# One product with ones per chunk, and output projections in fp16 parts, in a layer kernel on one core

## The chip, the cores and the metric

The kernel runs on one core of a Trainium2 chip. The core has TensorE (PE, matrix products; its weight loads are listed apart as PEld), VectorE (DVE), ScalarE (ACT), GpSimd (POOL) and the queues of SyncE (SP), from which most transfers are issued. The metric is the device time of one execution in microseconds. All times below are microseconds unless marked otherwise.

## What is computed

Two branches share one normalised input and are added to it (S = 2048 tokens, width D = 512):

```
xn = layernorm(x)
q = (xn @ wq) in 32 heads of 16;  k = xn @ wk;  v = xn @ wv      # one k and v for all heads
A  = concat_heads(softmax(q k^T / 4) v) @ wo                      # the output projection
s1, s2 = scores of xn against two sets of 64 keys, 32 heads       # product keys
top 2 of each, top 2 of the 4 sums, softmax g, expert index e
B  = sum over heads and 2 experts of g * gelu(xn . u[e]) * v[e]   # 4096 experts
out = x + A + B
```

For each token, branch B chooses 64 experts. Its choice must be the reference's, so the score products are exact to about fp32.

## The kernel before

**Split products.** A value that must stay near fp32 is scaled by a power of two and written as an fp16 high part plus an fp16 low part. ACT writes the high part (a copy with a scale), and DVE writes the low part (`scalar_tensor_tensor`: value times scale minus high part). One product of 128 x 128 x 512 is then three fp16 products into the same PSUM tile, the pairs (high, high), (high, low), (low, high) of `TERMS`. The queries, keys, scores and dense experts are done so. The power of two comes from `factors` (three integer operations on DVE) on a sum of squares. That sum is made with a product with a matrix of ones, which adds over the 128 partitions.

**The score weights.** The weights of the expert scores come in 8 chunks (`wp_make`), each of 4 parts. `wp_square` puts the squares of part n into one column of `squares` (128 x 4). `wp_factors` (L620 to L628) then adds the four columns with four fp32 products with ones, each with one moving column, into one PSUM column `pn`. ACT scales that by `K2`, and `factors` makes the chunk's scale. This happens 8 times, at 36 to 304 us.

**Attention.** Four query blocks of 512 tokens, in the order QB = (0, 1, 3, 2), times 8 groups of 4 heads, make 32 units. A unit runs over the 2048 keys in 16 pieces. For each piece PE makes scores (`sc`, L451), ACT their exponentials (`pt`, L458), and PE the product with the values and a column of ones (`pv`, L468, fp32). One step `d` of the main loop does two pieces; there are 256 steps, and `i` = 2d counts pieces. Two units are a pair `pp` (0 to 15). `unit_tail` copies the sums out, transfers place the rows in `ot` and the divisors in DRAM, `pair_load`, `pair_invert` and `pair_spread` invert and spread the divisors as `rs`, and `pair_tail` (L514 to L518), at remainder 12 of the next pair, multiplies `ot` by `rs` on DVE (L517). The product `on` has 128 rows of the attention output, fp32, transposed. Four pairs make one query block.

**Output projection.** `load_wo` fetches the weights `wo` (two tiles of 512 KB, fp32) once per query block. `block_out` (L562 to L576) multiplies 128 tokens: four fp32 products with `on` as weights and `wo` moving (L568), then DVE adds the PSUM tile to the token tile's total (L572). Twelve such blocks serve the first three query blocks of the order. The fourth is done at the end by `last_out_a` and `last_out_b`.

**Experts.** For half of the tokens, rows of u and v are gathered by index (POOL, L1194). For each row DVE makes a product with the token (L1206) and adds the weighted v row (L1241). For the other half (two groups of 512 tokens) the gates are spread into dense matrices by one-hot products (L988 to L1035), and all 4096 experts are run as dense products (`pact` L930, `pout` L1072).

**The order of the work.** It is written out in the program: the loop issues every engine's instructions step by step, and each engine runs its own in that order. In a step come the first two score products and exponentials, `pv`, then `mid()`, the other two scores, perhaps one `block_out`, and `fill()`. In `mid()`, functions put on `ON_ACT` in the step before or at the start of the step run on ACT, and functions put on `BEHIND` run on DVE among the sums of gathered rows. `store(...)` puts a transfer off to the start of the next step, on SP's queue. `fill()` runs the generator of the score and dense work (`score_thread`), which states a charge for each piece of work (`UNIT` = 0.235 per fp16 product, 3.6 per block). The generator is run until its charges reach an aim that rises evenly over the 256 steps to `FILL`. Gathered rows are issued at a rate per step that is set by the stage.

PSUM tiles of tag `x` (three buffers) serve scores, dense products, blocks and `pn`. Tag `wk` has 14 buffers of 2 KB per partition, tag `oh` three of 4 KB.

## Time and profile before

| | |
|---|---|
| three runs, median (lowest to highest) | 1775.51 (1774.38 to 1776.06) |
| the profiled execution | 1775.3 |
| its span, first to last instruction | 1773.3 |
| busy PE / DVE / ACT / POOL | 1687.8 / 1593.0 / 1329.7 / 680.2 |
| output blocks, PE (L568) | 96 records, 44.2 |
| products with ones (L625) | 64 records, 8.0 |
| products by the inverted sums (L517) | 15, 10.3 |

A row of groups has line, engine, operation, output<-inputs, shapes and count; then busy time and mean ns of one; then idle time of the engine just before and what ended it. A row of the timeline has start, duration, engine, line, operation and count. A row of the chain has start, length, engine, name, line and count; the chain is followed back from the last instruction, at each step to what released it. An fp32 product is two PE records. Durations of PE and DVE records overlap those of their neighbours, so the distance between starts, or the length in the chain, is what one instruction takes from a full engine.

### The profile page before, as it was taken

The page shows a single profiled execution, that of the slowest core. Times are in us where ns is not written, and L with a number is a line of the kernel's source. Part 1 is how long each engine was busy: PE and PEld are TensorE (multiplying, and loading weights), DVE is VectorE, ACT ScalarE, POOL GpSimd, SP SyncE. Part 2 cuts the span into 40 slices and gives each one's busy share as a digit, 9 for nine tenths or more (in the row PEclk, how much of TensorE's full clock was granted, in tenths as well). Part 3 has the DMA queues.
Part 4 walks back from the last instruction along what each step waited for, and adds up shares of the span by engine and source line. Part 5 has one row for each costly group of instructions (what it writes and reads, how often), then busy time and mean ns, then how long its engine had stood idle before and what let it go on. Part 6 is the DMA issues. An engine that isn't in the chain of part 4 may idle for free.

```text
span 1773.3 us, 35071 instructions
## 1 busy us (share of the span) xinstructions
PE 1687.8 (95%) x11070; PEld 597.5 (34%) x11070; DVE 1593.0 (90%) x6367; ACT 1329.7 (75%) x1793; POOL 680.2 (38%) x893
## 2 busy tenths in 40 slices
PE   7989998999998889999999999999998899999998
PEld 3433333333333333333333333333333333333332
DVE  7748898999999977999999999999999779999995
ACT  6467787877776988888988666666679877777774
POOL 1024454445542003444444445445520125455450
PEclk9999999999999999999999999999999999999999
DMA  7378879999773469999999977767544779999994
GB/s 272 120 251 313 273 267 309 303 323 336 256 257 103 158 220 280 330 334 337 332 338 360 357 264 240 236 222 230 177 126 137 235 235 330 327 311 345 321 311 146
DMA packets 257272, 470.97 MB, mean 266 GB/s; under 512 B 107316, under 2 KB 118596, under 8 KB 257084
## 3 DMA queue, kind: packets, MB, share of 16 engines
q0 software_dynamic: 73728, 268.47, 44.1%
q1 hardware_dynamic: 182940, 199.59, 34.7%
q8 instruction: 87, 1.43, 0.3%
q14 instruction: 101, 0.83, 0.1%
q10 hardware_dynamic: 416, 0.66, 0.1%
HBM read 407.36 MB, written 56.39 MB: 262 GB/s over the span
## 4 chain that ended last, share of the span: by engine, by line
PE 52%; DVE 30%; ACT 6%; issue 3%; DMA 1%; POOL 0%; SPq 0%; ACTq 0%; DVEq 0%; POOLq 0%
PE pv L468 16%; PE sc L451 9%; PE pout L1072 8%; PE pact L930 7%; DVE i L717 7%; PE psc L702 6%; DVE xa L1241 5%; DVE m L715 5%; DVE g L1206 4%; ACT pt L458 4%; DVE oh L988 3%; PE pwo L568 2%; PE pw L647 1%; DVE obs L991 1%; DVE obs L990 1%
## 5 line engine op out<-in xcount | busy, mean ns | idle before, releaser
L458 ACT ACTIVATE pt<-sc 128x1024 f32<-128x1024 f32 x1024 | 990.4, 1025 | 316.9 <-PE sc L451 269.8
L1194 POOL DMA_INDIRECT g<-in_uv_dram,idx x512 | 550.1, 1074 | 862.2 <-DVE xa L1241 395.3
L468 PE MATMUL pv<-pt,vaug 128*32 128x512 f32 x4096 | 495.0, 601 | 0.0
L1241 DVE SCALAR_TENSOR_TENSOR xa<-g,w,xa 128x512 f32<-128x512 f32 x512 | 374.0, 746 | 0.1
L702 PE MATMUL psc<-wk,xt 128*128 128x512 f16 x1536 | 356.4, 380 | 7.2 <-DVE wk L663 4.7
L451 PE MATMUL sc<-qa,kaug 64*128 64x512 f16 x2048 | 323.5, 383 | 36.3 <-ACT pt L458 29.5
L1206 DVE CUSTOM_DVE_ANT_0 g<-g,xa 128x512 f32<-128x512 f32 x512 | 334.6, 683 | 14.5 <-DMA g<-in_uv_dram,idx 14.2
L702 PEld LDWEIGHTS <-xt 128*128 128x128 f16 x1536 | 140.7, 98 | 204.1 <-issue 55.5
L451 PEld LDWEIGHTS <-kaug 64*128 64x128 f16 x2048 | 82.6, 94 | 373.9 <-issue 370.5
L717 DVE FIND_INDEX8 i<-m,psc 128x8 uint32<-128x64 f32 x1024 | 206.6, 224 | 0.0
L468 PEld LDWEIGHTS pv<-pt,vaug 128*32 128x32 f32 x4096 | 107.2, 109 | 253.5 <-issue 253.5
L930 PE MATMUL pact<-xt,wk 128*128 128x512 f16 x768 | 182.6, 383 | 0.0
L1072 PE MATMUL pout<-wk,wd 128*128 128x512 f16 x768 | 175.8, 379 | 0.0
L715 DVE MAX8 m<-psc 128x8 f32<-128x64 f32 x1024 | 146.2, 216 | 6.5 <-PE psc L702 6.2
L1072 PEld LDWEIGHTS <-wd 128*128 128x128 f16 x768 | 73.0, 98 | 92.6 <-issue 8.1
L930 PEld LDWEIGHTS <-wk 128*128 128x128 f16 x768 | 69.1, 98 | 99.9 <-issue 26.7
L988 DVE TENSOR_TENSOR oh<-io,tr 128x2048 f16<-128x2048 f16 x64 | 78.0, 1218 | 4.9 <-PE pg L1026 4.8
L717 DVE MATCH_VALUE_LOAD i<-m,psc 128x8 f32 x1024 | 74.3, 73 | 0.0
L761 POOL CAST fi<-i 128x64 f32<-128x64 uint32 x30 | 7.7, 257 | 145.6 <-DVE i L717 142.0
L1075 DVE SCALAR_TENSOR_TENSOR da<-pout,cols,da 128x512 f32<-128x512 f32 x72 | 53.0, 744 | 5.9 <-PE pout L1072 5.4
L1145 DVE SCALAR_TENSOR_TENSOR gy<-gy,pact 128x512 f32<-128x512 f32 x60 | 40.8, 680 | 17.3 <-ACT gy L1144 17.0
L880 DVE SCALAR_TENSOR_TENSOR wk<-rw,cols,wk 128x512 f16<-128x512 f32 x64 | 47.5, 745 | 6.9 <-ACT wk L877 6.9
(227 smaller groups left out, 1451.9 us busy)
## 6 DMA issues: line engine op xcount, KB each, us to landing
wk<-dw SPq DMA_DIRECT2D x96, 256.0 KB
wqt<-in_wqT_dram SPq DMA_DIRECT2D x32, 512.0 KB
un<-in_uv_dram SPq DMA_DIRECT2D x16, 1024.0 KB
ds<-wk SPq DMA_DIRECT2D x64, 256.0 KB
gates<-dg SPq DMA_DIRECT2D x64, 256.0 KB
wk<-ds SPq DMA_DIRECT2D x64, 256.0 KB
dg<-gst SPq DMA_DIRECT2D x14, 928.0 KB
dw<-wk SPq DMA_DIRECT2D x32, 256.0 KB
```

What stands on the lines that cost most here:

```text
L451: nc.tensor.matmul(p[:, b, :], kaug[o:o + 64, kc * P:(kc + 1) * P], QA[u][o:o + 64, i, :], start=True, stop=True)
L458: nc.scalar.activation(PT[u, kc, i], p, AF.Exp, scale=SCALE)
L468: nc.tensor.matmul(PV[u][32 * j:32 * j + 32, :], vaug[:, kc, :], pt[:, b, :], start=kc == 0, stop=kc == 15)
L702: nc.tensor.matmul(p, XT[kk][:, a, j * P:(j + 1) * P], WC[n_][kk][:, bb, :], start=n == 0, stop=n == 11)
L715: nc.vector.max(m8[:, jb, s, :], p[:, s * E:(s + 1) * E])
L717: nc.vector.max_index(i8[:, jb, s, :], m8[:, jb, s, :], p[:, s * E:(s + 1) * E])
L930: nc.tensor.matmul(p, us[:, a, k * P:(k + 1) * P], XT[k][:, c, :], start=n == 0, stop=n == 11)
L988: nc.vector.tensor_tensor(out=oa, in0=num(P), in1=bc(0, tb, P), op=OP.is_equal)
L1072: nc.tensor.matmul(p, wd[0][:, a, j * P:(j + 1) * P], vs[:, c, :], start=n == 0, stop=n == last)
L1194: nc.gpsimd.indirect_dma_start(out=gt, out_offset=None, in_=uv, in_offset=bass.IndirectOffsetOnAxis(ap=IDX[ph, c, ti][:, s:s + 1], axis=0))
L1206: nc.vector.tensor_tensor_reduce(u, u, XN[TPH * ph + ti], scale=1.0, scalar=0.0, op0=OP.mult, op1=OP.add, accum_out=a[:, i:i + 1])
L1241: nc.vector.scalar_tensor_tensor(acc, v, w[:, i:i + 1], acc, op0=OP.mult, op1=OP.add)
```

## The change

Two things are changed.

1. `wp_factors` makes one product with ones over all four columns of `squares` (two records). DVE adds the four results (`reduce_sum`) and multiplies by `K2`; the ACT instruction goes.

2. The output projections of the first three query blocks are done in fp16 parts. `wo` is loaded at step 48, squared on ACT (steps 50 and 51), given a factor (step 53: one product with ones, `factors`, and the factor `C_WO` that undoes all scales), split into high and low parts at steps 54 to 57, and stored in DRAM as `d_wo`; `load_wo` reads it from there, as many bytes as before. `pair_tail` of the first twelve pairs multiplies in place in `ot` and then makes high and low parts of `on`: the high one on ACT through `ON_ACT` in the next step, the low one on DVE through `BEHIND`. `block_out` runs 12 fp16 products, and its add on DVE is a `scalar_tensor_tensor` with `C_WO`. The charge of a block becomes 2.7 and `FILL` 937.2. The last query block stays fp32.

```diff
-FILL = 948.0
+FILL = 937.2
...
+    d_wo = dram.tile([P, KC, 2, 512], F16, name="dwo")
...
+        nc.vector.tensor_scalar(col(S_O), col(S_WKV), 1.0 / 32.0, None, op0=OP.mult)
...
     def pair_tail(pp):
-        rs = RB.pop(pp)
-        on = late[0].tile([P, 512], F32, name="on", tag="on", bufs=5)
-        nc.vector.tensor_mul(on, OT.pop(pp), rs)
+        rs, ot = RB.pop(pp), OT.pop(pp)
+        if pp > 11:
+            on = late[0].tile([P, 512], F32, name="on", tag="on", bufs=5)
+            nc.vector.tensor_mul(on, ot, rs)
+        else:
+            on = late[0].tile([P, 2, 512], F16, name="on", tag="on", bufs=5)
+            nc.vector.tensor_mul(ot, ot, rs)
+
+            def high():
+                nc.scalar.activation(on[:, 0, :], ot, AF.Copy, scale=col(S_O))
+                behind(lambda: nc.vector.scalar_tensor_tensor(on[:, 1, :], ot, col(S_O), on[:, 0, :],
+                                                              op0=OP.mult, op1=OP.subtract))
+
+            on_act(high)
         ON[pp] = on
+    def wo_raw():
+        NU["wo"] = [big.tile([P, 2, D], F32, name="wor", tag="oh", bufs=3) for _ in range(2)]
+        for h, w in enumerate(NU["wo"]):
+            nc.sync.dma_start(w, wo[2 * h * P:2 * (h + 1) * P, :].rearrange("(k p) n -> p k n", p=P))
+
+    def wo_square(h):
+        junk = big.tile([P, 2, D], BF16, name="junk", tag="wk", bufs=NWK)
+        nc.scalar.activation(junk, NU["wo"][h], AF.Square, accum_out=wo_sums[:, h:h + 1])
+
+    def wo_factors():
+        p = xtile("pn")[:, :2]
+        nc.tensor.matmul(p, ones_f, wo_sums, start=True, stop=True)
+        x = small.tile([P, 1], F32, name="xw")
+        nc.vector.reduce_sum(x, p, axis=AX.X)
+        nc.vector.tensor_scalar(x, x, 2.0, None, op0=OP.mult)
+        factors(x.bitcast(I32), col(S_WO), col(I_WO))
+        nc.vector.scalar_tensor_tensor(col(C_WO), col(I_KV), 32.0 * XUP * XUP, col(I_WO), op0=OP.mult, op1=OP.mult)
+
+    def wo_split(k):
+        raw_, w = NU["wo"][k // 2][:, k % 2, :], wk_tile()
+        nc.scalar.activation(w[:, 0, :], raw_, AF.Copy, scale=col(S_WO))
+        behind(lambda: nc.vector.scalar_tensor_tensor(w[:, 1, :], raw_, col(S_WO), w[:, 0, :],
+                                                      op0=OP.mult, op1=OP.subtract))
+        store(lambda: store(lambda: nc.sync.dma_start(d_wo[:, k], w)))
...
+    def wo_steps(d):
+        if d == 48:
+            wo_raw()
+        if d in (50, 51):
+            on_act(lambda: wo_square(d - 50))
+        if d == 53:
+            wo_factors()
+        if 54 <= d < 58:
+            on_act(lambda: wo_split(d - 54))
...
     def block_out():
...
         for k in range(KC):
-            nc.tensor.matmul(p, ON[4 * m + k][:, j * P:(j + 1) * P], WO[k // 2][:, k % 2, :],
-                             start=k == 0, stop=k == KC - 1)
+            for a, c in TERMS:
+                nc.tensor.matmul(p, ON[4 * m + k][:, a, j * P:(j + 1) * P], WO[k // 2][:, k % 2, c, :],
+                                 start=n == 0, stop=n == 11)
+                n += 1
...
-        behind(lambda: nc.vector.tensor_add(acc, acc, p))
+        behind(lambda: nc.vector.scalar_tensor_tensor(acc, p, col(C_WO), acc, op0=OP.mult, op1=OP.add))
...
     def wp_factors():
-        p = xtile("pn")[:, :1]
-        for h in range(4):
-            nc.tensor.matmul(p, ones_f, squares[:, h:h + 1], start=h == 0, stop=h == 3)
+        p = xtile("pn")[:, :4]
+        nc.tensor.matmul(p, ones_f, squares, start=True, stop=True)
         x = small.tile([P, 1], F32, name="xw")
-        nc.scalar.activation(x, p, AF.Copy, scale=col(K2))
+        nc.vector.reduce_sum(x, p, axis=AX.X)
+        nc.vector.tensor_mul(x, x, col(K2))
         factors(x.bitcast(I32), col(S_W + c), col(I_W + c))
...
-                    yield 3.6
+                    yield 2.7
...
-            spent[0] += 3.6
+            spent[0] += 2.7
...
             norm_steps(d)
+            wo_steps(d)
             att_steps(d, mid, fill)
```

## The prediction

> **What bounds the kernel now.** I read the page's busy times first, then the busy time by stage (cut where the chain of waits changes engine), then the chain piece by piece, then single instructions.

> ```profile
> span 1773.3 us, 35071 instructions
> PE 1687.8 (95%) x11070; PEld 597.5 (34%) x11070; DVE 1593.0 (90%) x6367; ACT 1329.7 (75%) x1793; POOL 680.2 (38%) x893
> PE 52%; DVE 30%; ACT 6%; issue 3%; DMA 1%; POOL 0%; SPq 0%; ACTq 0%; DVEq 0%; POOLq 0%
> ```
> Two engines are nearly full, and the chain changes between them. By stage (columns: window, length, then busy time of PE, weight loads, DVE, ACT, POOL):

> ```profile
> 121.00:319.00 198.00, 185.67 (x1157) 64.61 (x1157) 174.44 (x887) 159.18 (x233) 90.71 (x115) 0.99 0.85 287
> 319.00:563.00 244.00, 236.35 (x1466) 80.68 (x1464) 240.06 (x1527) 183.40 (x252) 113.71 (x208) 1.00 0.83 278
> 563.00:650.00 87.00, 74.34 (x894) 30.75 (x894) 81.82 (x142) 77.35 (x96) 4.53 (x4) 0.96 0.45 152
> 650.00:700.00 50.00, 49.09 (x305) 16.59 (x302) 30.60 (x72) 39.96 (x52) 10.29 (x10) 1.00 0.86 279
> 1000.00:1147.00 147.00, 146.62 (x876) 49.23 (x874) 142.22 (x810) 93.09 (x113) 75.28 (x97) 1.00 0.78 270
> 1147.00:1315.00 168.00, 167.59 (x1037) 56.71 (x1036) 164.67 (x1082) 106.50 (x131) 81.96 (x158) 1.00 0.60 196
> 1405.00:1500.00 95.00, 94.79 (x558) 31.81 (x556) 73.08 (x181) 73.17 (x96) 30.82 (x29) 1.00 0.85 264
> ```
> In 650 to 700 and 1405 to 1500 PE alone is full. In 319 to 563 both are, but DVE's 4 us of idle are smaller than PE's 7.6, and the chain there is DVE's own work, one instruction behind another:

> ```profile
> by line: DVE i L717 30.1%; DVE m L715 19.7%; DVE xa L1241 18.2%; DVE g L1206 15.8%; issue 1.7%; DVE wk L663 1.1%; DVE gy L1216 0.9%; DVE mx L748 0.9%; DVE gd L815 0.9%; DVE cond L745 0.8%; DVE da L819 0.7%; DVE mx L747 0.7%; DVE gq L1215 0.
> ```
> The chain of 1147 to 1315 is the same kind; in the two stretches of one-hot products (563 to 650, 1315 to 1405) it is mostly DVE too. So a microsecond taken from PE counts in one place, and one given to DVE in another.

> **The change, part by part.**

> *The output blocks.* Each of the 12 blocks has 4 fp32 products, two records each; afterwards 12 fp16 products of the size that L930 and L1072 run already.

> ```profile
> 661.50 3.60 PE L568 MATMUL pwo<-wo,on 128*128 128x512 f32 x8
> 667.96 2.76 PE L930 MATMUL pact<-xt,wk 128*128 128x512 f16 x12
> 661.67 3.43 PE pwo L568 x8
> 713.84 2.59 PE pout L1072 x12
> 1063.60 3.63 PE pwo L568 x8
> 1492.14 3.63 PE pwo L568 x8
> L572 DVE TENSOR_TENSOR xa<-xa,pwo 128x512 f32<-128x512 f32 x8 | 5.4, 681 | 0.5 <-PE pwo L568 0.5
> L1075 DVE SCALAR_TENSOR_TENSOR da<-pout,cols,da 128x512 f32<-128x512 f32 x72 | 53.0, 744 | 5.9 <-PE pout L1072 5.4 <-issue 0.4
> L1072 PEld LDWEIGHTS <-wd 128*128 128x128 f16 x768 | 73.0, 98 | 92.6 <-issue 8.1
> ```
> The first two rows are the timeline, the next four the chain, which holds all 12 blocks, the last three groups of the whole run. 3.44 becomes 2.59: 0.85 saved, times 12 is 10.2. Four blocks lie at 661 to 690 and four at 1413 to 1495, with DVE far from full: 6.8 in full. The middle four (1063 to 1105) save 3.4, but DVE must keep up, and its only wait in 1000 to 1125 that PE can shorten is this one:

> ```profile
> DVE w L1229 <- ACT gth L1222: 3.2, 2, 2.4
> 333.62 1.99 DVE xa L1241 x3
> ```
> Three full-width scalar_tensor_tensor take 1.99 in the chain: 0.664 each. One new one falls at 1107, so 2.5 of the 3.4 counts. Bounds: 0 and 3.4. **Gain 9.3.** The add at L572 becomes a scalar_tensor_tensor from PSUM, 0.681 to 0.744: 12 times 0.063, nearly all where DVE has room, 0.

> *One product with ones per chunk.*

> ```profile
> 302.88 0.95 PE L625 MATMUL pn<-squares,ones_f 128*128 128x1 f32 x8
> L625 PE MATMUL pn<-squares,ones_f 128*128 128x1 f32 x64 | 8.0, 246 | 0.0
> L627 ACT ACTIVATE xw<-pn,cols 128x1 f32<-128x1 f32 x8 | 2.1, 260 | 3.0 <-PE pn L625 2.9
> ```
> Eight records start 0.10 to 0.11 apart ((0.95 - 0.25)/7); two remain. Six records less, eight times: 48 x 0.11 = 5.3. In 121 to 319, where six of the eight lie, PE stands idle for 12 of 198 us behind ACT and DVE, and some of what it gains it will wait away. Bounds 0 and 5.3; I take three quarters, **4.0**, since the chain there is mostly PE's. ACT loses 8 x 0.26 and its wait; DVE gets two small instructions, 8 x 2 x 0.135 (spacing below) = 2.2, of which I count a seventh, **0.3**, about DVE's share of the chain there. The wait for PE that ACT had is now DVE's: behind it stand the gathered rows' sums, and for them POOL's gathers. DVE runs behind PE there (the next rows show it for the same kind of product), so it finds the product done: 0.

> ```profile
> 528.06 0.28 PE L1351 MATMUL pn<-um,ones_f 128*128 128x2 f32 x2
> 535.85 0.15 DVE L1353 TENSOR_SCALAR ux<-pn 128x2 f32<-128x2 f32 x1
> 536.66 0.15 DVE L1358 SCALAR_TENSOR_TENSOR cols<-ui 128x1 f32<-128x1 f32 x1
> ```
> Seven small instructions in 0.81 between first and last start: 0.135 each; and DVE came 7.8 us after PE.

> *Splitting the attention rows.* Twelve pair_tail calls add one ACT instruction (as L877) and one on DVE (as L880):

> ```profile
> L877 ACT ACTIVATE wk<-rw,cols 128x512 f16<-128x512 f32 x64 | 44.2, 727 | 0.0
> L880 DVE SCALAR_TENSOR_TENSOR wk<-rw,cols,wk 128x512 f16<-128x512 f32 x64 | 47.5, 745 | 6.9 <-ACT wk L877 6.9
> L517 DVE TENSOR_TENSOR on<-ot,rsb 128x512 f32<-128x512 f32 x15 | 10.3, 686 | 0.9 <-DMA rsb<-dinv 0.8
> L1206 DVE CUSTOM_DVE_ANT_0 g<-g,xa 128x512 f32<-128x512 f32 x64 | 42.5, 683 | 0.0
> ```
> (The last row is of 319 to 563 alone.) By the places of L517, two of the twelve DVE ones fall into 319 to 563 (398.7, 500.8), two into 1147 to 1315, one into each one-hot stretch, one at 281.8 where ACT and DVE are both loaded, the rest where DVE has some room. With 0.664 each: counted with the next item; **1.3**; **1.3**; at 281.8 with its ACT part **1.0**; the rest **0.3**.

> *Splitting the weights once* (steps 48 to 57, about 451 to 515). DVE: 4 x 0.664 and six small ones 0.8; with the two lows above 6 x 0.664 + 0.8 = **4.8** on the DVE chain of 319 to 563. ACT: two squares and four copies, some 5 us, beside ACT's 60 us of idle there. SP: two loads of 512 KB, four stores of 256 KB; the stores wait for DVE's low and behind them stand SP's loads of weights and rows. At 278 GB/s the 2 MB are 7.5 us of transfer, hidden as long as gathered rows still come early: DVE's L1206 waited 0.0 there. Without that cover, up to 7.5. The product with ones holds one of the three PSUM tiles until DVE comes; PE waits, inside its 7.6 idle.

> *The new wait on ACT.* The high part waits for DVE's product in L517, and behind it on ACT stand the exponentials, for which PE's scores wait.

> ```profile
> 394.88 1.02 ACT L458 ACTIVATE pt<-sc 128x1024 f32<-128x1024 f32 x1
> 398.74 0.67 DVE L517 TENSOR_TENSOR on<-ot,rsb 128x512 f32<-128x512 f32 x1
> 1393.59 1.94 ACT L458 ACTIVATE pt<-sc 128x1024 f32<-128x1024 f32 x2
> 1399.23 0.69 DVE L517 TENSOR_TENSOR on<-ot,rsb 128x512 f32<-128x512 f32 x1
> 1404.43 0.62 PE L1026 MATMUL pg<-obs,oh 128*128 128x64 f16 x16 [1.58 <-DVE obs L991]
> ```
> At 398.74 ACT has done the step's second exponential at 395.90 and would stand until 399.41: 3.5. Read in the same way the waits are 3.1 (500.8), 0.8 (900.7), 0.2, 2.1, 1.8 and 4.4 (1399.2), none at the other five: 15.9 in all. Those of 319 to 563 and 1147 to 1315 delay PE where DVE sets the pace: 0. At 1399 PE loses some 2.8, of which 1.58 is a wait it has anyway: **1.2**; **0.5** at 900, **0.3** at 597. Bounds: 0 and all 15.9.

> *FILL.* The allowance of score work for each of 256 steps is (FILL - 14.9)/256, 14.9 by the charges in the code: 3.645 becomes 3.603. Block charges fall by the same 10.8 in all, so the sum is unchanged, but before the first blocks work runs late: 0.75 step at step 64. That brings 1.7 more gathered rows (2.3 a step by the code; 0.664 for the sum, 0.6 for the product, 0.14 for a share of the small ones) into 319 to 563: 2.4.

> ```profile
> 1119.47 1.85 PE pv L468 x16
> 1121.33 0.54 PE sc L451 x4
> ```
> Later steps are missing in return: 0.19 in the first dense part and 0.56 after 1000, each with 1.85 + 2 x 0.54 = 2.9 of PE's attention work: 2.2 back. **0.2.**

> *Sum*: -9.3 - 4.0 + 0.3 + 1.3 + 1.3 + 1.0 + 0.3 + 4.8 + 1.2 + 0.5 + 0.3 + 0.2 = **-2.1**. The profiled execution took 1775.3, its span and 2.0 around it, which is 0.2 under the median of 1775.51. It gives 1773.2 in its own terms, 1773.4 in the median's. The bounds of the product with ones alone move this by -1.3 and +4.0, those of the middle four blocks by -0.9 and +2.5.

> The trace weighs PE by its chain. [...]

> **The rivals.**

> A, faster: *DVE's stretches have room after all.* PE is as full as DVE in 1147 to 1315 (167.59 of 168) and nearly so in 319 to 563; if PE sets the pace, the 4.8, 1.3 and 1.3 lie beside its work. 1773.4 - 7.4 = 1766.0. Against it: the chain does not touch PE there.

> B, slower: *the exponentials queue behind the new wait.* The 15.9 of ACT's standing still reach PE, because ACT serves both buffers of scores. If 60% passes, 9.5 less the 2.0 counted: 1773.4 + 7.5 = 1780.9. From 2.0 + 5.7 = 7.7 of 15.9 on (half), the kernel is slower than no change by 0.2%. For it: PE already waits for L458 at places. Against it: 10.5 of the 15.9 lie where PE has slack.

> C, slower: *DVE sets the end everywhere*, PE's gain is worth nothing. 16 x 0.664 + 12 x 0.063 + 23 x 0.135 = 14.5: 1790. Against it: 30.60 busy of 50 beside four blocks that are on the chain.

> D, it doesn't do what it says: *each of the 12 fp16 products pays its weight load* (0.098 by L1072's loads), 3.77 a block, 0.33 more than before: 1773.4 + 9.3 + 4.0 = 1786.7. Against it: 12 in 2.59, with loads, in the chain.

> **How the numbers follow.** Forecast 0.48 with 1769 to 1778 of its own, A 0.26, B 0.19, C 0.04, D 0.03. A measurement of this kernel tells about 0.2% (3.6 us) from no change: faster is below 1772.0, slower above 1779.1. Of the forecast 0.17 lies below, 0.02 above; of A 0.25 below; of B 0.14 above, with C and D 0.07. So faster 0.42, same 0.35, slower 0.23. The range reaches to A with its upper pn bound (1764) and to B (1782).

> **What would show it.** Right: pwo groups of 12 in 2.6 on the chain; two pn records a chunk; PE's idle in the first dense stretches unchanged; the stretch from the last transposed weights (319) to the first one-hot product longer by 4 to 8 us, its chain still DVE; at the high copies ACT's exponentials late by 2 to 4 us without a PE wait of that size. Wrong: that stretch as long as before (A), waits of scores for L458 grown by over 6 us in all (B), or pwo above 3 us (D).

## The result, and the profile after

The changed kernel took 1801.15 (median; 1797.92 to 1802.78), the kernel before beside it 1775.47 (1774.38 to 1776.06): a recorded ratio of 1.0114, interval 1.0082 to 1.0145 (the two medians alone make 1.0145). By the medians it is slower by some 26, by the ratio by some 20, where 2.1 less was forecast. The profiled execution of the kernel after took 1802.78, its span is 1801.1.

The page of the kernel after (busy times, and the chain's shares by engine):

```profile
span 1801.1 us, 35130 instructions
PE 1686.2 (94%) x11072; PEld 591.2 (33%) x11072; DVE 1609.2 (89%) x6406; ACT 1336.3 (74%) x1805; POOL 677.4 (38%) x893
PE 46%; DVE 30%; ACT 8%; DMA 4%; issue 4%; SPq 0%; POOL 0%; ACTq 0%; DVEq 0%; POOLq 0%
```

PE is as busy as before (1686.2 against 1687.8) in a span that is 27.8 longer. DVE's share of the chain has not moved; ACT and DMA, 6% and 1% before, have 8% and 4%. So the time went into PE's waiting, not into the engine that got more work.

Busy time by stage, cut at the same events in both kernels: first product with the values, last transposed weights, first one-hot product, last of the first group of them, end of the first dense stretch, the second group of one-hot products, last product with the values. Columns as in the prediction; the last three are the granted clock, the busy share of the DMA engines and GB/s. Before, three of the seven rows and the sum of all:

```profile
121.50:326.40 204.90, 191.78 (x1198) 67.22 (x1196) 181.16 (x922) 164.76 (x241) 92.04 (x116) 0.99 0.85 289
326.40:570.30 243.90, 236.09 (x1457) 79.90 (x1454) 237.57 (x1502) 181.72 (x249) 111.88 (x207) 0.99 0.80 269
655.90:970.50 314.60, 304.85 (x1837) 102.84 (x1833) 285.70 (x666) 268.55 (x370) 124.49 (x113) 1.00 0.97 326
sum 1635.70, PE 1574.48 PEld 545.93 DVE 1507.62 ACT 1261.52 POOL 664.81; mean PE 224.93 PEld 77.99 DVE 215.38 ACT 180.22 POOL 94.97
```

and after:

```profile
123.20:339.10 215.90, 194.30 (x1186) 64.34 (x1185) 187.63 (x946) 167.23 (x241) 92.01 (x118) 0.97 0.82 284
339.10:584.70 245.60, 235.13 (x1435) 79.93 (x1434) 239.04 (x1510) 184.10 (x254) 116.86 (x208) 0.99 0.80 274
674.30:1000.00 325.70, 306.18 (x1852) 102.53 (x1849) 291.58 (x680) 270.98 (x374) 127.30 (x115) 0.98 0.95 321
sum 1660.60, PE 1571.33 PEld 540.36 DVE 1522.75 ACT 1268.09 POOL 661.96; mean PE 224.47 PEld 77.19 DVE 217.54 ACT 181.16 POOL 94.57
```

Two stages carry the loss, 11.0 and 11.1: the first, and the first dense stretch. The stage of which the forecast said that it would grow by 4 to 8 (here the second row) grew by 1.7. Over all stages PE stood idle for 1635.70 - 1574.48 = 61.2 before and 89.3 after: 28.1 more. Its busy time fell by only 3.2, though the blocks (10.2) and the products with ones (4.0 for the six chunks in this time) took some 14 from it. The reason is in the clock column: 0.97 and 0.98 where it was 0.99 and 1.00.

**The clock.** Three cuts of 2 us of the kernel after:

```profile
816.00:818.00 2.00, 1.62 (x16) 0.43 (x9) 1.94 (x8) 1.93 (x5) 0.00 (x0) 1.00 1.01 400
818.00:820.00 2.00, 0.00 (x0) 0.00 (x0) 1.70 (x4) 2.00 (x4) 0.94 (x1) 1.00 0.26 88
...
822.00:824.00 2.00, 2.00 (x14) 0.59 (x16) 2.00 (x6) 2.00 (x4) 1.39 (x2) 0.50 0.86 195
```

and the chain of waits there:

```profile
819.58 1.83 ACT pt L460 x2
...
822.07 3.57 PE pv L470 x16
```

PE waits 2.9 for exponentials, and for the 6.8 that follow its clock is half: sixteen products with the values take 3.57, where the prediction's rows have 1.85. The wait is paid twice: 2.9 of standing, and by estimate some 3 more for the 6.8 at half clock. In the profiles of the kernel before and after such a stretch is 3.41 long, or a multiple (6.83 at 820.15; only the one at the execution's end is shorter, 2.65 and 3.32), and in each profile all lie on one grid: the starts at 192.61 and 1319.01 of the kernel before are 1126.40 apart, 330 times 3.413. After the first product with the values, and leaving out the execution's last one, the kernel before has four, at 192.61, 564.66, 646.58 and 1319.01; the kernel after has eleven, at 175.04, 198.93, 332.05, 410.56, 516.37, 707.51, 820.15 (two together), 1239.99, 1345.81 and 1427.73. Some of them, cut out:

```profile
175.04:178.45 3.41, 3.41 (x18) 0.64 (x20) 1.19 (x4) 2.52 (x3) 0.00 (x0) 0.50 0.95 346
...
410.56:413.97 3.41, 3.41 (x18) 0.56 (x12) 3.41 (x23) 1.34 (x3) 2.79 (x3) 0.50 1.03 341
...
1239.99:1243.40 3.41, 3.19 (x18) 0.69 (x17) 3.41 (x20) 1.99 (x3) 2.80 (x8) 0.50 0.02 5
```

Seven more of them, 3.41 each at half speed with PE nearly full, are some 12 of PE time. The account of PE's busy time then nearly closes: 12 more for the half clock and 14 less work make 2 less, where it fell by 3.2. With the 28.1 more of idle time that is the 24.9 by which the stages together grew.

The waits that grew or are new (who waited for whom: microseconds in total, times, the longest). Before:

```profile
PE sc L451 <- ACT pt L458: 29.5, 57, 1.4
```

and after:

```profile
PE sc L453 <- ACT pt L460: 54.0, 90, 2.9
ACT on L526 <- DVE ot L523: 19.2, 8, 4.2
ACT wk L934 <- DMA rw<-in_ub_dram: 5.4, 2, 3.7
```

The timeline of ACT after, at three of the high parts (in brackets the idle time before, and what ended it):

```profile
406.37 0.72 ACT L526 ACTIVATE on<-ot,cols 128x512 f16<-128x512 f32 x1 [2.39 <-DVE ot L523]
512.22 0.72 ACT L526 ACTIVATE on<-ot,cols 128x512 f16<-128x512 f32 x1 [3.40 <-DVE ot L523]
1237.61 0.72 ACT L526 ACTIVATE on<-ot,cols 128x512 f16<-128x512 f32 x1 [4.24 <-DVE ot L523]
```

and that of PE, at three of its waits:

```profile
174.37 1.36 PE L704 MATMUL pw<-wqt,kTs 128*64 128x512 f32 x4 [3.13 <-DVE xw L683]
332.62 1.09 PE L717 MATMUL pwt<-ident,wt 128*128 128x128 f32 x4 [2.85 <-DVE i L774]
...
1239.30 0.47 PE L453 MATMUL sc<-qa,kaug 64*128 64x512 f16 x2 [2.21 <-ACT pt L460]
```

Six of the eleven half-clock stretches begin within 6 us of a high part (at 406, 512, 703, 1237, 1342, 1424). Near the one at 1342 the kernel before has a half-clock stretch too, at 1319.01; the other five are new. Of the rest, that at 175.04 comes behind the wait for DVE to read the sum of the product with ones, and that at 332.05 behind a transpose that waits for DVE. What was to be seen of the blocks is there, two records of `pn` a chunk (16 records in all) and the blocks on the chain in 2.59 to 2.70 each where they were 3.43 to 3.63:

```profile
1442.60 2.59 PE pwo L624 x12
1519.23 2.70 PE pwo L624 x12
```

### The profile page after: what moved, and what is told of

Same layout as the page of the kernel before. It is cut to its first block, busy times and chain, and to the rows that moved or that the text cites. A ratio compares the mean times of both kernels' runs of the same rounds, so it can differ in the third digit from the quotient of the medians.

```text
span 1801.1 us, 35130 instructions
## 1 busy us (share of the span) xinstructions
PE 1686.2 (94%) x11072; PEld 591.2 (33%) x11072; DVE 1609.2 (89%) x6406; ACT 1336.3 (74%) x1805; POOL 677.4 (38%) x893
## 4 chain that ended last, share of the span: by engine, by line
PE 46%; DVE 30%; ACT 8%; DMA 4%; issue 4%; SPq 0%; POOL 0%; ACTq 0%; DVEq 0%; POOLq 0%
PE pv L470 15%; PE sc L453 8%; PE pout L1129 8%; DVE i L774 7%; PE pact L987 6%; PE psc L759 6%; ACT pt L460 6%; DVE xa L1298 5%; DVE m L772 5%; DVE g L1263 4%; DVE oh L1045 1%; PE pw L704 1%; PE pwo L624 1%; DMA rw<-in_ub_dram 1%; DMA gates<-dg 1%
## 5 line engine op out<-in xcount | busy, mean ns | idle before, releaser
L470 PE MATMUL pv<-pt,vaug 128*32 128x512 f32 x4096 | 503.2, 610 | 0.0
L453 PE MATMUL sc<-qa,kaug 64*128 64x512 f16 x2048 | 326.4, 385 | 56.8 <-ACT pt L460 54.0
L759 PE MATMUL psc<-wk,xt 128*128 128x512 f16 x1536 | 357.3, 380 | 10.3 <-DVE wk L720 8.4
L759 PEld LDWEIGHTS <-xt 128*128 128x128 f16 x1536 | 141.2, 98 | 205.3 <-issue 56.3
L1129 PEld LDWEIGHTS <-wd 128*128 128x128 f16 x768 | 73.1, 98 | 92.6 <-issue 8.2
L987 PEld LDWEIGHTS <-wk 128*128 128x128 f16 x768 | 69.2, 98 | 100.3 <-issue 28.1
L1045 DVE TENSOR_TENSOR oh<-io,tr 128x2048 f16<-128x2048 f16 x64 | 77.9, 1216 | 10.2 <-PE pg L1083 9.2
L774 DVE MATCH_VALUE_LOAD i<-m,psc 128x8 f32 x1024 | 69.5, 68 | 0.0
```

The source lines that it names most:

```text
L453: nc.tensor.matmul(p[:, b, :], kaug[o:o + 64, kc * P:(kc + 1) * P], QA[u][o:o + 64, i, :], start=True, stop=True)
L470: nc.tensor.matmul(PV[u][32 * j:32 * j + 32, :], vaug[:, kc, :], pt[:, b, :], start=kc == 0, stop=kc == 15)
L759: nc.tensor.matmul(p, XT[kk][:, a, j * P:(j + 1) * P], WC[n_][kk][:, bb, :], start=n == 0, stop=n == 11)
L774: nc.vector.max_index(i8[:, jb, s, :], m8[:, jb, s, :], p[:, s * E:(s + 1) * E])
L987: nc.tensor.matmul(p, us[:, a, k * P:(k + 1) * P], XT[k][:, c, :], start=n == 0, stop=n == 11)
L1045: nc.vector.tensor_tensor(out=oa, in0=num(P), in1=bc(0, tb, P), op=OP.is_equal)
```

## The experiments

Each kernel is timed against the kernel before on its own chip, and these differ between the groups, so ratios are compared. The last column is the mean over the kernel's runs of the granted clock of each; the kernel before had 0.992 to 0.993 beside them.

| kernel | median (lowest to highest) | ratio (interval) | clock |
|---|---|---|---|
| the change | 1801.15 (1797.92 to 1802.78) | 1.0114 (1.0082 to 1.0145) | 0.9885 |
| pn_alone | 1779.68 (1776.42 to 1788.72) | 0.9998 (0.9973 to 1.0023) | 0.9926 |
| blocks_alone | 1802.25 (1800.60 to 1803.01) | 1.0116 (1.0064 to 1.0167) | 0.9855 |
| high_later | 1798.61 (1796.37 to 1803.08) | 1.0107 (1.0054 to 1.0159) | 0.9878 |
| pn_act | 1797.31 (1793.59 to 1801.75) | 1.0103 (1.0072 to 1.0135) | 0.9867 |
| fill_moved | 1792.99 (1791.13 to 1796.20) | 1.0079 (1.0058 to 1.0099) | 0.9920 |
| fill_kept | 1791.41 (1783.53 to 1799.09) | 1.0068 (1.0031 to 1.0104) | 0.9890 |
| kept_later | 1786.61 (1784.62 to 1795.70) | 1.0051 (1.0021 to 1.0080) | 0.9905 |
| kept_later_act | 1780.34 (1776.72 to 1789.24) | 1.0013 (0.9983 to 1.0044) | 0.9905 |
| kept_fp32 | 1794.71 (1792.76 to 1803.33) | 1.0082 (1.0052 to 1.0113) | 0.9885 |
| part_fp16 | 1781.00 (1777.69 to 1786.45) | 0.9993 (0.9972 to 1.0015) | 0.9919 |
| part_oldpn | 1781.29 (1779.84 to 1793.21) | 1.0009 (0.9988 to 1.0030) | 0.9922 |
| before_again | 1780.30 (1776.92 to 1785.32) | 0.9999 (0.9983 to 1.0015) | 0.9934 |
| wo_only | 1782.64 (1778.56 to 1791.80) | 1.0014 (0.9995 to 1.0034) | 0.9912 |
| fill_half | 1796.48 (1794.18 to 1800.47) | 1.0101 (1.0070 to 1.0131) | 0.9898 |
| fill_up | 1786.44 (1783.47 to 1797.04) | 1.0053 (1.0026 to 1.0080) | 0.9915 |
| late_up | 1790.51 (1784.10 to 1794.63) | 1.0058 (1.0038 to 1.0078) | 0.9896 |
| low_pool | 1782.67 (1775.18 to 1789.64) | 1.0006 (0.9986 to 1.0026) | 0.9905 |
| late_dve | 1787.39 (1783.69 to 1792.02) | 1.0035 (1.0017 to 1.0053) | 0.9896 |

### The two parts, each alone

**pn_alone** is the kernel before with the new `wp_factors`; **blocks_alone** is the kernel after with the old one.

```diff
 # blocks_alone, against the kernel after
-        p = xtile("pn")[:, :4]
-        nc.tensor.matmul(p, ones_f, squares, start=True, stop=True)
+        p = xtile("pn")[:, :1]
+        for h in range(4):
+            nc.tensor.matmul(p, ones_f, squares[:, h:h + 1], start=h == 0, stop=h == 3)
...
-        nc.vector.reduce_sum(x, p, axis=AX.X)
-        nc.vector.tensor_mul(x, x, col(K2))
+        nc.scalar.activation(x, p, AF.Copy, scale=col(K2))
```

> The kernel before with the new wp_factors alone (one product with ones, its four columns added on DVE; the ACT instruction gone). Theory T, that DVE comes several us later than ACT did to read the PSUM tile of the product, and that PE waits for the tile: 1779 to 1784, slower than before by 4 to 8. The prediction's term (PE's 5.3 us saved, three quarters of it on the path): 1771 to 1772. Rival: it is neutral, 1774 to 1777, and all of the loss is in the output projections.

> The changed kernel with the old wp_factors: the output projections alone. Theory Q, that the new wait of ACT for DVE's product (19.2 us in eight waits in the trace of the changed kernel) delays the exponentials and through them PE: 1790 to 1798, most of the loss of 26. The prediction's sum without the product with ones: 1777. Rival: the loss is mainly of the product with ones, then 1776 to 1783.

Measured: 0.9998 and 1.0116. The product with ones alone shows neither the 4.0 of the prediction nor a loss; its interval, some 4.5 to either side, just reaches the 4.0. The profile of pn_alone is clearer. In the stretch where six of the eight products lie (first product with the values to last transposed weights), PE is busy for 186.4, against 191.8 and 190.4 in two profiles of the kernel before, and idle for 19.1, against 13.1 and 14.9; the stretch is 205.5 long, against 204.9 and 205.3. With the blocks, their splits, their waits and the moved `FILL`, and without the new product with ones, the whole loss is there.

### The new wait, and the late reader

**high_later** puts the high part on ACT a step later, when DVE's product has long been done. **pn_act** lets ACT read the four sums and DVE add them from SBUF, so that the PSUM tile is not held until DVE comes.

```diff
 # high_later
-            on_act(high)
+            LATER_ACT.append(high)
 # pn_act
-        nc.vector.reduce_sum(x, p, axis=AX.X)
-        nc.vector.tensor_mul(x, x, col(K2))
+        xs = small.tile([P, 4], F32, name="xs")
+        nc.scalar.activation(xs, p, AF.Copy, scale=col(K2))
+        nc.vector.reduce_sum(x, xs, axis=AX.X)
```

> The changed kernel with the high part put on ACT one step later, when DVE's product is done; no work is added or removed. Theory Q: ACT's waits for the product fall from 19.2 to under 3 us and the time to 1780 to 1788. Rival, that the work added on DVE makes the loss wherever ACT does its part: 1797 to 1802.

> The changed kernel in which ACT reads the product with ones (four columns, scaled by K2, into SBUF) and DVE adds the four from there, so the PSUM tile is freed by ACT as in the kernel before, with one product as in the changed one. Theory T: 1792 to 1797, faster than the changed kernel by 4 to 9. Rival, that the tile's reader does not matter: 1799 to 1802.

Measured: 1.0107 and 1.0103, against 1.0114: within the intervals neither shows a gain. In high_later ACT no longer waits for the product, and the five new half-clock stretches named above are gone. Two double ones came at 538.47 and 729.62, behind other waits, so that nine remain of eleven. The waits that did not come from it stayed or grew:

```profile
PE sc L453 <- ACT pt L460: 48.1, 83, 4.5
...
ACT wk L934 <- DMA rw<-in_ub_dram: 10.8, 4, 6.0
```

The exponentials still come late in the first dense stretch, now because ACT's copies of the experts' weights stand ahead of them and wait for their rows. So neither cause explains the loss alone.

### FILL and the charge, alone and taken back

**fill_moved** is the kernel before with nothing but `FILL` and the charge of the change. **fill_kept** is the kernel after with the old ones.

```diff
 # fill_moved, against the kernel before
-FILL = 948.0
+FILL = 937.2
...
-                    yield 3.6
+                    yield 2.7
...
-            spent[0] += 3.6
+            spent[0] += 2.7
```

> The kernel before with FILL 937.2 and a charge of 2.7 per block, nothing else: the score work falls into the steps as in the changed kernel, with fp32 blocks and no splitting. Theory F, that the steps 28 and 29 (10.9 and 9.2 in all kernels with 937.2, 5.9 and 7.0 in those with 948) and what follows from them are due to this alone: slower than before by 6 to 15. Rival, that it only moves waits from one step to the next (the prediction's 0.2): within 3 of the kernel before.

> The changed kernel with FILL 948 and a charge of 3.6, as before: the score work falls into the steps as in the kernel before. Theory F: faster than the changed kernel by 6 to 15, 1786 to 1795. Rival, that the loss is of the new wait and the added work: 1797 to 1803.

Measured: 1.0079 for the move alone, with not one product, copy or transfer changed, some 14; taking it back in the changed kernel brings 1.0114 to 1.0068, some 8, which is no more than the uncertainty of that difference. By the first figure, the term that the prediction put at 0.2 is half of the loss or more. Its first place is seen in the steps at which the last transposed weights are made. The windows of those two steps, in fill_moved and then in before_again (below), the kernel before:

```profile
318.60:329.70 11.10, 8.25 (x50) 3.20 (x50) 8.74 (x41) 6.40 (x10) 4.05 (x4) 0.85 0.86 299
329.70:338.70 9.00, 6.90 (x45) 2.45 (x43) 7.75 (x42) 5.24 (x9) 4.93 (x12) 1.00 0.91 297
```

```profile
322.50:328.40 5.90, 5.90 (x47) 2.52 (x47) 5.90 (x26) 5.90 (x9) 1.39 (x2) 1.00 0.77 270
328.40:335.40 7.00, 7.00 (x48) 2.42 (x50) 6.86 (x40) 5.10 (x9) 4.74 (x11) 1.00 0.94 307
```

Two steps take 20.1 where they take 12.9. With the other charge the first of them holds 12 records of score products and 8 of transposes, where the kernel before has 9 and 8. The chain of fill_moved shows what that does:

```profile
319.53 1.02 ACT pt L458
320.54 0.10 ACT gth L1222
...
322.91 0.66 DVE xa L1241
...
323.65 1.05 DVE m L715 x8
324.70 1.61 DVE i L717 x8
326.31 0.14 issue
326.45 1.09 PE pwt L660 x4
327.54 1.28 PE psc L702 x3
328.81 0.56 PE sc L451 x2
```

It is a ring: the exponential, behind it on ACT the gathered rows' `gth`, behind that DVE's sums, behind them DVE's search for the best scores, which frees the PSUM tile for the transposes, behind which PE makes the next scores for the exponential. PE's clock falls with it (0.85); over the whole execution, though, the mean clock of fill_moved is that of the kernel before beside it (0.9920 and 0.9921). The count of products alone doesn't decide whether the ring closes: the step before these two has 12 and 8 in the kernel before and takes 7.5. The other place is the first dense stretch. There PE's waits for the exponentials come to 6.7 before, 17.2 in fill_moved and 18.1 in the kernel after; the waits of that stretch before, and after:

```profile
PE sc L451 <- ACT pt L458: 6.7, 11, 1.4
```

```profile
PE sc L453 <- ACT pt L460: 18.1, 25, 2.9
```

In it the DMA engines are nearly always busy (share 0.95 to 0.97 above), and transfers stand on the chain of waits, longer than before. The longest one there of the kernel before, and two of the kernel after:

```profile
804.65 6.98 DMA rw<-in_ub_dram
```

```profile
756.15 11.45 DMA gates<-dg
...
846.65 10.59 DMA rw<-in_ub_dram
```

`FILL` is not all that lengthens this stretch. In the twelve profiles with `FILL` 948 it takes 311.8 to 316.8 in seven and 320.2 to 325.4 in five. The longest of these is pn_alone's, where nothing in the stretch is changed:

```profile
659.10:984.50 325.40, 309.40 (x1838) 103.33 (x1834) 286.05 (x666) 269.15 (x370) 124.84 (x113) 0.98 0.95 316
```

All six profiles with 937.2 or 942.6 have 324.3 to 328.8. So with the old `FILL` the longer form of this stretch comes and goes between executions; in every profile with a lower one it was there. What starts it stays open.

### The mends together

**kept_later** is fill_kept with the high part a step later; **kept_later_act** adds ACT's reading of the sums. The edits are those shown above.

> FILL 948 and a charge of 3.6, and the high part on ACT one step later. If the two causes are F and the new wait, and nothing else, the loss is gone and the prediction's gain is left: 1772 to 1782. If the dense part at full DMA load loses again what was won ahead of it, as with the high part later alone: 1785 to 1792.

> The same, and ACT reads the product with ones. If the reader of the tile matters at this place of the work too: 4 to 8 under the run with DVE as reader. If it mattered only with FILL 937.2, where step 7 took 11.9 with DVE and 7.4 with ACT: within 3 of it.

Measured: 1.0068, 1.0051, 1.0013. With all three mended the changed kernel is as fast as the kernel before, within the interval. The steps of 0.0017 and 0.0038 are about 3 and 7, each within the spread of its kernels, so their sizes are rough. A gain over the kernel before is still not seen.

### Where the blocks' gain went

**kept_fp32** is kept_later_act with every block as four fp32 products over the same tiles. **part_fp16** is kept_later_act with the first query block as in the kernel before, so that only eight pairs are split. **part_oldpn** is that with the old product with ones. **before_again** is the kernel before. The output projections of kept_fp32, and of wo_only below, are not the reference's: they read the bits of split parts as fp32, with `S_O` made smaller.

```diff
 # kept_fp32, against kept_later_act
-        nc.vector.tensor_scalar(col(S_O), col(S_WKV), 1.0 / 32.0, None, op0=OP.mult)
+        nc.vector.tensor_scalar(col(S_O), col(S_WKV), 2.0 ** -18, None, op0=OP.mult)
...
-            for a, c in TERMS:
-                nc.tensor.matmul(p, ON[4 * m + k][:, a, j * P:(j + 1) * P], WO[k // 2][:, k % 2, c, :],
-                                 start=n == 0, stop=n == 11)
+            nc.tensor.matmul(p, ON[4 * m + k].bitcast(F32)[:, j // 2, j % 2 * P:(j % 2 + 1) * P],
+                             WO[k // 2].bitcast(F32)[:, k % 2, :, :], start=k == 0, stop=k == KC - 1)
 # part_fp16, against kept_later_act
-        if pp > 11:
+        if pp > 11 or pp < 4:
...
-            load_wo(i == STEPS - 10)
+            load_wo(i in (138, STEPS - 10))
```

> The kernel with the old FILL and charges, the high parts a step later and ACT reading the sum (1780.3 in its own run), but with each block as 4 fp32 products over the same tiles read as fp32 (8 records of 0.43): all splits, waits and transfers stay, only the 12 blocks of PE go back to 3.44. Its output projection is not the reference's. Theory (the blocks' gain arrives at the end, and the splits cost as much as it brings): 9 to 10 above the kernel with fp16 blocks, about 1790. Rival (the gain on PE is made good elsewhere, by transfers in the first dense stretch or by DVE): within 3 of it, 1778 to 1784.

> The same mended kernel, but the first query block stays as before (its four pairs are not split, its four blocks are fp32), so four of the twelve splits go, three of them in the stretches where DVE sets the pace, and a third of the gain. Theory (a split costs 2.5 to 5 where DVE sets the pace, as the steps of the earlier runs show at 39, 55 and 71): 11 less for the splits, 3.4 more for the blocks, about 1773, below the kernel before. Rival (what a split delays is made good by the time the first dense stretch ends): 1780 to 1784.

> As the one before it, with the product with ones as it was (four products, ACT reads the one column). Theory (the product with ones is worth nothing by itself when ACT reads it, as it was when tried alone): within 2 of the one before it. Rival (the six records fewer on PE are worth the 4.0 of the prediction once DVE doesn't hold the tile): 4 above it.

> The kernel before once more, as a control on this chip: ratio 1.000, and a profile of it here. Theory: its first dense stretch (700 to 1000) takes about 303 as in the first profile, with no wait of ACT's weight copies for their rows over 1 us. Rival: the stretch of 9 us lost at steps 113 to 121, seen in three of the profiles on this chip, comes in it too, and is then no part of the change.

Measured: 1.0082, 0.9993, 1.0009 and 0.9999. From kept_fp32 to kept_later_act the ratio falls by 0.0069, about 12, and by the two intervals anything from 5 to 20: the blocks' gain does arrive, at a size that agrees with the 10.2 of 12 times 0.85. It is seen most plainly in the last stage, from the second group of one-hot products to the last product with the values, which holds four blocks. In kept_fp32 and in kept_later_act:

```profile
1421.90:1775.50 353.60, 350.30 (x2131) 117.38 (x2127) 308.56 (x764) 271.04 (x359) 148.10 (x136) 1.00 0.87 295
```

```profile
1421.80:1770.80 349.00, 346.74 (x2142) 115.86 (x2142) 307.60 (x764) 269.63 (x357) 148.60 (x136) 1.00 0.88 299
```

With `FILL` 948, all five profiles with fp32 blocks there have 352.1 to 353.6, and all seven with fp16 blocks 348.8 to 350.2; four blocks at 0.85 are 3.4. But kept_fp32, which has all the rest of the change and not the gain, lies 0.0082 above the kernel before, so all that is done for the blocks costs as much as they bring. part_fp16 went as its rival said: four splits fewer did not bring 11, and with 0.9993 it is not told apart from the kernel before, nor from part_oldpn. The control has no long wait of ACT's weight copies (1.3 at most). A single one of 5.6 to 6.3 near 910 stands in four other profiles, of kept_later, kept_later_act, wo_only and pn_alone, and these are four of the five with the longer dense stretch above. In pn_alone neither `FILL` nor a split is changed, and I can't say what starts it.

### What the splits cost, and whether FILL has an order

**wo_only** is kept_fp32 without the twelve splits of the attention rows. **fill_half** and **fill_up** are the kernel before with a charge of 3.15 and 4.05 and `FILL` of 942.6 and 953.4; **late_up** is kept_later_act with the latter pair.

```diff
 # wo_only, against kept_fp32
-        if pp > 11:
+        if True:
...
 # fill_up, against the kernel before
-FILL = 948.0
+FILL = 953.4
...
-            spent[0] += 3.6
+            spent[0] += 4.05
```

> The mended kernel with fp32 blocks (1794.7), and without the twelve splits of the attention rows: only the weights are split and stored, and the product with ones changed. Its output projection reads the split weights' bits as fp32 and is not the reference's. Theory (the twelve splits on DVE and ACT are what costs): 1780 to 1783, as the kernel before. Rival (the split of the weights and its 2 MB of transfers cost most of the 13): 1788 to 1795.

> The kernel before with the charge of a block halfway (3.15) and FILL 942.6, so that the sum of charges is the same; nothing else. Theory (late score work costs in proportion): half of the 14 of the full move, about 1787. Rival (what matters is which pieces of work fall into one step, and that has no order): any value between 1778 and 1795, most likely near one end.

> The kernel before with the charge moved the other way (4.05, FILL 953.4): score work earlier by 0.75 step at step 64. Theory (lateness costs in proportion, earliness gains or is worth nothing): 1768 to 1780. Rival (any move away from the arrangement that was there costs, since the steps' contents change): 1785 to 1795.

> The mended kernel (high parts a step later, ACT reads the sum, fp16 blocks) with charge 4.05 and FILL 953.4. Theory (earlier score work gives the splits room): below its 1780.3, 1770 to 1780, a version that beats the kernel before. Rival: 1785 to 1795, as any move.

Measured: wo_only 1.0014, so the twelve splits cost 0.0068, about 12, one microsecond each on average (6 to 18 in all by the intervals). Taking them out also changes what falls together in a step, as `FILL` does, and that share was not separated. The split of the weights, its 2 MB of transfers and the new product with ones are 2 or 3 together, within the interval of nothing. `FILL` at charges 2.7, 3.15, 3.6 and 4.05 gives 1.0079, 1.0101, 0.9999 and 1.0053: no order, and the rival holds. Half of the move costs no less than the whole, and the move the other way costs too, also in the mended kernel (1.0058 against 1.0013). So it isn't lateness alone that costs: each of the three other arrangements of the same work is slower than that at 948. In the profiles of fill_moved and fill_half PE is idle for 73.5 and 72.2 over the stages, against 61.2 and 66.9 in the two of the kernel before. In fill_up, with 65.7, it is not idle longer, but it stands at half clock for 20.5, against 13.7 and 10.2.

### ACT's share and DVE's share of a split

**low_pool** lets GpSimd subtract the low part; DVE's product by the inverted sums takes the scale as well. **late_dve** lets DVE make the high part too.

```diff
 # low_pool, against kept_later_act
-            nc.vector.tensor_mul(ot, ot, rs)
+            nc.vector.scalar_tensor_tensor(ot, ot, col(S_O), rs, op0=OP.mult, op1=OP.mult)
...
-                nc.scalar.activation(on[:, 0, :], ot, AF.Copy, scale=col(S_O))
-                behind(lambda: nc.vector.scalar_tensor_tensor(on[:, 1, :], ot, col(S_O), on[:, 0, :],
-                                                              op0=OP.mult, op1=OP.subtract))
+                nc.scalar.copy(on[:, 0, :], ot)
+                behind(lambda: nc.gpsimd.tensor_tensor(on[:, 1, :], ot, on[:, 0, :], op=OP.subtract))
```

> The mended kernel (1780.3), with the low part of the attention rows made by GpSimd instead of DVE: DVE multiplies by the inverted sums and the scale in one instruction, ACT copies, GpSimd subtracts. Theory (DVE's 12 x 0.664 is most of what the splits cost): 8 less, about 1772, a version that beats the kernel before. Rival (GpSimd's issue of gathers behind the subtraction is delayed, or ACT's share is what costs): 1779 to 1786.

> The mended kernel (1780.3), with the high part made by DVE instead of ACT, right behind the product by the inverted sums. Theory (DVE's share is what costs): 12 x 0.7 more on DVE, 1786 to 1790. Rival (ACT's share, and its wait for DVE, is what costs): 1774 to 1779.

Measured: 1.0006 and 1.0035. Against kept_later_act, twelve more instructions on DVE cost some 4 (0.0022), and twelve fewer brought some 1 (0.0007); both are within the intervals. late_dve lies above the kernel before, beyond its interval, and kept_later_act does not. So DVE's share may be part of the price, but taking it off DVE was not seen to return it. In low_pool the list of waits puts 69.2 of GpSimd's idle time, in six places, down to ACT's copy, with the gathers in the queue behind; how much of it kept gathers back was not separated:

```profile
POOL on L527 <- ACT on L526: 69.2, 6, 51.5
```

No version that was run beats the kernel before beyond its interval.

## Why the prediction was wrong

**The blocks: -9.3, right.** Groups of 12 in 2.59 to 2.70, about 12 (5 to 20) between kept_fp32 and kept_later_act, and 3 to 4 in the stage of the last four blocks. Rival D is out. So is rival C's view that PE's gain is worth nothing: PE's matrix time is what these two kernels differ in.

**The product with ones: -4.0, not seen.** Two records a chunk, but 0.9998 alone. The prediction let three quarters of PE's saving through in a stretch where, as it said itself, PE stands idle behind ACT and DVE; in the profile of pn_alone PE's idle time there grew by as much as its work fell. That DVE "finds the product done: 0" looked at DVE's wait and not at the tile: in the kernel after `pn` was done at 168.1, DVE read it at 174.2, and PE's next product of the weights stood 3.13 for the tile and then ran at half clock from 175.04. What that costs by itself is not shown, since ACT as the reader (pn_act) brought 1.0103 against 1.0114. The sentence on PE waiting inside its idle time was written of the weights' one product; for the eight of the chunks it was not asked.

**The splits: mis-sized.** The twelve low parts and their ACT parts were in the sum with about 5 (the 4.8 less 3.5 for the weights, and 1.3, 1.3, 1.0, 0.3); measured 12 (6 to 18). The split of the weights was in with 3.5 and measured, with the product with ones, 2 or 3. That a low part is nearly free where DVE has some room does not fit this; what it delays in such places was not separated.

**The new wait: read well, carried on wrongly.** 15.9 were read off for seven places; there were 19.2 in eight. The prediction said that waits where DVE sets the pace cost nothing and counted 2.0. PE's waits for the exponentials grew by 24.5, over the 6 that it named as the sign of rival B, and the five new half-clock stretches follow high parts, three of them in the two stretches where it counted 0. Rival B is right in kind. The time that its wait costs by itself came out at 1 and 3 in the two pairs run, each uncertain by 8 or more, so B's 7.5 is not excluded; in high_later other waits took its place. That this wait alone made the loss is excluded by high_later.

**FILL: 0.2, the step that failed worst.** It counted how much work is late and what that work takes, and found no net cost. The runs show 14 for the move alone (10 to 18 by its interval) and, less surely, 8 for taking it back, without order in the size of the move. At the last transposed weights the runs show how: other pieces fall into one step together and two steps take 20.1 for 12.9, and a sum of durations cannot see that. In the first dense stretch, the other place, the cause stays open.

**What the sum had no term for: the clock.** A wait of PE was priced at its length. The rows in the prediction held the other half (0.96 in the stretch of one-hot products), and it was not asked what made it. By the stage account of the two profiles it is some 12 of the 25. The mean clock over the kernels' runs, 0.9885 against 0.992 to 0.993 for the kernel before beside the experiments, would make it 6 to 8.

The stretch from the last transposed weights grew by 1.7 in the kernel after, nearer to A's sign than to the forecast, but by 6.1 in kept_later_act (330.4 to 580.4, against 326.4 to 570.3), where `FILL` is kept: the forecast of 4 to 8 held for that arrangement. A's time, 1766, was seen in no kernel. Rival C (1790) fell: DVE's share of the chain is 30% as before, it is PE's idle time and clock that grew.

## What to carry to other kernels

In a schedule written out by hand, a new instruction is to be priced by what waits behind it and by which tile it holds, on each queue it enters, before its duration; three microseconds of waiting at one point cost PE some five here, by estimate (3.13, and half of the 3.41 at half clock that follow at 175.04). A constant that only paces the work is an edit of its own: try it alone, and keep it while another edit is measured. Where a saving on the fullest engine needs a little work on all the others, compare the saving with the price that such work has had at the same places, not with the instruction's length.

## What was not expected of the hardware

**The spread between runs goes with it.** kept_later_act ran from 1776.72 at a mean granted clock of 0.994 to 1789.24 at 0.986. Over the 16 runs of the kernel before beside the first experiments, time and clock are correlated with -0.87, 2.2 us for each 0.001 (1.6 to 2.5 beside the other experiments); 0.001 of 1775 is 1.8, by estimate what the lower clock costs where PE is always full. Whether the waits themselves add to it is not shown. Which comes first in a run was not separated: no experiment changed the clock alone.
